# An indirect row transfer with 96 rows in place of 97, in a fused attention, Fourier and expert kernel

## The chip, the cores and the metric

The kernel runs on one core of one Trainium2 chip. The metric is the device time of one execution in microseconds (us). The core's engines are TensorE (PE), VectorE (DVE), ScalarE (ACT), GpSimd (POOL) and SyncE (SP, which here only issues transfers); each has its own instruction queue and works it off in order, and they wait for each other and for transfers by semaphores. Sixteen DMA engines carry the transfers.

## What is computed

Three parts follow each other, all in float32. Shapes: 4 batches, 8 heads, 576 tokens, head size 64, so a model width of 512; 32 memory slots; 8 experts.

```python
# attention through 32 memory slots
a = softmax(phi, axis=tokens)
k_m, v_m = einsum(a, k), einsum(a, v)                # (32, 64) for each head
attn = softmax(q @ k_m.T / 8)
x = heads_side_by_side(attn @ v_m)                   # (4, 576, 512)
# Fourier mix, then a dense feed-forward network (FFN)
u = x + real(fft(fft(x, axis=tokens), axis=model))
un = layer_norm(u)
x = u + relu(un @ w_ch1) @ w_ch2                     # 512 -> 2048 -> 512
# experts: one expert for each token, by a gate and a scan along the tokens
out[t] = p[e] * (relu(x[t] @ w1[e]) @ w2[e])         # 512 -> 1024 -> 512
```

## The kernel before

The kernel has three stages. The first (0 to about 207 us) does attention and the Fourier mix batch by batch, and meanwhile loads and prepares the weights of the FFN. The second runs the FFN over 9 groups of 256 tokens. The third runs the experts, with loops whose length the chip decides.

In the first stage the real part of the transform over the tokens is symmetric: the rows s and -s (that is 576 - s) use the same products. So for each batch b only the tokens 0 to 288 are worked, in three row blocks t = 0, 1, 2 of 97, 96 and 96 rows (`ROWS`: tokens 0-96, 97-192, 193-288), one row in each SBUF partition. The function `mix` (L495) finishes a block. It forms `ta` and `tb` (the difference and the sum of two halves of a PSUM tile, L503 and L504) and from them two result tiles:

- `ut0`, the rows s themselves. They are in order and go by ordinary transfers, issued on SP, into the segment t of `u[b]` in DRAM (L515). `spread` cuts such a transfer into the rows that make a multiple of 16 and the rest, so 97 rows go as 96 and 1.
- `ut1`, the rows -s (written by L510 and L511 in the second pass of the loop at L507). They come out in reverse order and go by one indirect transfer, issued on POOL (L520), into the segment 5 - t of `u[b]`. The list of target rows is the column t of `mi`, one number in each partition, made on the host in `constants` (L92 to L98). Two rows have no mirror image, token 0 (the first row of t=0) and token 288 (the last row of t=2); their number is 2^20, out of the bounds that the transfer is given, and such a row is not written.

The segments (`SEGS`) have 97, 96, 96, 95, 96 and 96 rows.

`ut0` and `ut1` have two buffers each. L510 of a block therefore waits until the transfer of the block two before it has left its buffer: t=2 waits for t=0's, the next batch's t=0 for t=1's.

The order of all instructions on each engine is fixed when the program is built. The loop bodies are generators that state which engine they need, for how long and after what; `weave` (L215) picks the step that starts earliest by those stated times, and what it issues is then in the engine's queue for good. For the landing of an indirect transfer it assumes 2.6 us after the issue (L519), whatever the row count.

Right behind `mix` on DVE's queue stand, from case to case, the preparation of weights (`sw`, L640 to L644), the scaled `kb` and `vb` of the next batch (L417), and in the last batch `hl`, the low half of the FFN's hidden values (L1030). PE needs `kb` for L427, and then ACT, PE and DVE follow with L430, L441, L444, L480 and `mx` (L486). The products of the FFN are at L989 to L991: `pl` of the first layer, `y` of the second. After the third block of batch 2, SP fetches the first token group's rows from `u` (L268), and DVE starts on them at L298.

Of the kernel before, what the change touches and what calls it, by code (L numbers as in the profile page):

```python
# [18 lines left out]
IO = bass.IndirectOffsetOnAxis  # L19

B, H, S_, D = 4, 8, 576, 64
# [9 lines left out]
SEGS = ((0, 97), (97, 96), (193, 96), (289, 95), (384, 96), (480, 96))  # L31
# [49 lines left out]
def constants():  # L81

    s = np.arange(289)
    ang = 2 * np.pi * np.outer(s, s) / S_
    c = np.cos(ang)
    c[0] *= 0.5
    c[288] *= 0.5
    n = np.sin(ang)
    n[[0, 288]] = 0
    n[:, [0, 288]] = 0  # L90
    cs = np.zeros((112, 3, 2, 289), np.float32)
    midx = np.full((112, 3), 1 << 20, np.int32)  # L92
    for t, (o, m) in enumerate(ROWS):
        cs[:m, t, 0] = c[o:o + m]
        cs[:m, t, 1] = n[o:o + m]
        for r in range(m):
            if 1 <= o + r <= 287:
                midx[r, t] = S_ - (o + r) - SEGS[5 - t][0]  # L98
    d = PERM[:, None] * np.arange(257)[None] * 2 * np.pi / DM
    cd = np.concatenate([np.cos(d), np.sin(d[:, 1:256])], 1).astype(np.float32)  # L100
    cd = np.ascontiguousarray(cd.reshape(4, 128, 512).transpose(1, 0, 2))
    p = np.arange(128)
    s0 = np.zeros((128, NT))
    for b in range(B):
        s0[S_ * b % 128, S_ * b // 128] = 1
    f = {
        "s0": s0,
        "tid": 128 * np.arange(NT)[None] + p[:, None] - N,
        "desc": np.tile(8 - np.arange(8), (128, 1)),
        "iotaC": np.tile(np.arange(256), (128, 1)),  # L110
        "ohR": (p[:, None] // 9 == np.arange(8)[None]) & (p[:, None] < 72),
        "kR": np.where(p < 72, p % 9, 0)[:, None],
        "ones": np.ones((128, 8)),
        "ident": np.eye(128),
        "mask": np.kron(np.eye(4), np.ones((32, 1))),
        "half": np.full((128, 1), -0.5),
        "k256": np.tile(256 * np.arange(9), (128, 1)),
        "row": p[:, None],
        "big": np.tile([768, -768], (128, 1)),
    }  # L120
    c1, c2 = (np.concatenate([f[n] for n, _ in x], 1).astype(np.float32) for x in FIELDS)
    return {"cs": cs, "cd": cd, "c1": c1, "c2": c2, "midx": midx}
# [36 lines left out]
def attention_fourier_experts_kernel(ctx, tc, qT, phi, kv, w1, w2, wg, wgc, wm, cs, cd, c1, c2, midx, out):  # L159
    nc = tc.nc  # L160
    V, S, T, G = nc.vector, nc.scalar, nc.tensor, nc.gpsimd
# [3 lines left out]
    u = [[dram.tile([n, DM], F32, name=f"u_{b}_{r}") for r, n in SEGS] for b in range(B)]  # L165
# [35 lines left out]
    def ended(*names):  # L201
        return [end.get(n, 0.0) for n in names]
# [49 lines left out]
    def spread(rows):  # L252

        n = rows - rows % 16
        return [(a, b) for a, b in ((0, n), (n, rows)) if b > a]
# [80 lines left out]
    mi = ac.tile([112, 3], I32, name="mi")  # L336
# [158 lines left out]
    def mix(b, t, xp, pq, pq_end):  # L495

        o, m = ROWS[t]
        r = yield "S", 0.27, [pq_end]
        S.copy(qs[:m, 1:256], pq[:m, 257:512])
        ta = aw.tile([97, 257], F32, name="ta")  # L500
        tb = aw.tile([97, 257], F32, name="tb")
        r = yield "V", 0.68, [r]
        V.tensor_tensor(out=ta[:m], in0=pq[:m, 0:257], in1=qs[:m], op=ALU.subtract)  # L503
        V.tensor_tensor(out=tb[:m], in0=pq[:m, 0:257], in1=qs[:m], op=ALU.add)  # L504
        mark["D"] = 3 * b + t
        end["D", 3 * b + t] = r
        for hf, (e, f) in enumerate(((ta, tb), (tb, ta))):  # L507
            ut = aw.tile([97, 512], F32, name=f"ut{hf}", bufs=2)
            r = yield "V", 0.68, ended(("sent", 3 * b + t - 2, hf))
            V.tensor_tensor(out=ut[:m, 0:256], in0=xp[hf][:m, 0:256], in1=e[:m, 0:256], op=ALU.add)  # L510
            V.tensor_tensor(out=ut[:m, 256:512], in0=xp[hf][:m, 256:512], in1=f[:m, 1:257], op=ALU.add)  # L511
            if hf == 0:
                end["sent", 3 * b + t, 0] = yield "D", 0.55, [r]
                for p, q in spread(m):
                    nc.sync.dma_start(out=u[b][t][p:q], in_=ut[p:q])  # L515
        end["mix", 3 * b + t] = r
        if t < 2 or b + 1 < B:
            mark["mix"] = 3 * b + t
        end["sent", 3 * b + t, 1] = 2.6 + (yield "G", 1.04, [r])  # L519
        G.indirect_dma_start(out=u[b][5 - t], out_offset=IO(ap=mi[:m, t:t + 1], axis=0), in_=ut[:m],  # L520
                             in_offset=None, bounds_check=SEGS[5 - t][1] - 1, oob_is_err=False)
        mark["mix"] = 3 * b + t

# [2 lines left out]
    def mixer():  # L526
        for n in range(3 * B):
            yield lambda: len(mixes) > n
            yield float(BATCH["mix"][n // 3])
            yield from mix(*mixes[n])  # L530
# [753 lines left out]
```

## Time and profile before

| | before |
|---|---|
| median of 3 runs | 925.37 us (923.09 to 926.46) |
| the profiled execution | 925.92 us |
| its span (first to last instruction) | 924.2 us |
| PE busy | 827.2 us (90%) |
| DVE busy | 617.2 us (67%) |
| ACT busy | 317.3 us (34%) |
| POOL busy | 214.7 us (23%) |
| software queue of the transfers (q0) | 7472 packets, 14.02 MB |

The profile is that of one execution. All times in it are counted from the start of the span. The busy shares are means over the three stages: PE's 90% is 144.63 us of the first 207 and 473.24 us of the 483 us from 207 to 690 us. What one stage is worth is read from its own rows. An indirect transfer appears twice: as POOL's time to issue it, and as a landing, the time from the start of the issue to the last row's arrival. Where the profile could tell a landing for sure, it gives one.

### The profile page before, as it was taken

To read this page: it belongs to the slowest core of one execution; us is meant where nothing else is said; L and a number is where in the kernel's file an instruction comes from. 1 tells how busy PE (TensorE), PEld (TensorE's weight loads), DVE (VectorE), ACT (ScalarE), POOL (GpSimd) and SP (SyncE) were. 2 spreads that over 40 slices of the span, in tenths; PEclk is the share of its full clock that TensorE was granted. 3 is DMA by queue.
4 is the path that set the end of the run, shared out by engine and by line. 5 is a ranking of instruction groups with operands and counts; after the bars stand their busy time and mean duration, and the time that the engine had idled before them with its cause. 6 is when DMAs were issued, how large, how long until landed. Compare 5 with 4: busy or idle time off the path is not lost. (4 is left out here: it accounts for less than half of the span.)

```text
span 924.2 us, 14424 instructions
## 1 busy us (share of the span) xinstructions
PE 827.2 (90%) x5296; PEld 703.4 (76%) x5296; DVE 617.2 (67%) x1422; ACT 317.3 (34%) x595; POOL 214.7 (23%) x179
## 2 busy tenths in 40 slices
PE   5594959568899999999999999999998998999993
PEld 2353636357789989898989898988987997889973
DVE  3984956469987665757575757577865666766654
ACT  3452624235431111111111111115344555645543
POOL 0544544337410000000000000003323331333330
PEclk9787978799899999999999999999998999999997
DMA  9865632344240100000000000019366667866665
GB/s 333 280 216 148 242 88 64 102 141 147 76 164 1 47 24 24 24 24 24 23 25 24 24 23 18 6 56 356 132 212 209 218 220 264 285 222 232 223 214 188
DMA packets 38714, 123.43 MB, mean 134 GB/s; under 512 B 8096, under 2 KB 8352, under 8 KB 36826
## 3 DMA queue, kind: packets, MB, share of 16 engines
q1 hardware_dynamic: 29880, 103.22, 33.5%
q0 software_dynamic: 7472, 14.02, 4.7%
q10 hardware_dynamic: 1266, 4.98, 1.5%
q8 instruction: 52, 0.85, 0.4%
q14 instruction: 44, 0.36, 0.1%
HBM read 107.41 MB, written 15.57 MB: 133 GB/s over the span
## 5 line engine op out<-in xcount | busy, mean ns | idle before, releaser
L991 PE MATMUL pl<-xh,w1l 128*128 128x256 f32 x864 | 243.3, 282 | 0.0
L989 PE MATMUL pl<-xh,w1h 128*128 128x256 f32 x576 | 163.5, 284 | 3.7 <-DVE hl L1030 3.7
L991 PEld LDWEIGHTS pl<-xh,w1l 128*128 128x128 f32 x864 | 164.5, 190 | 0.0
L990 PE MATMUL pl<-xl,w1h 128*128 128x256 f32 x576 | 161.8, 281 | 0.0
L1028 ACT ACTIVATE hh<-pl 128x256 fp32r<-128x256 f32 x144 | 55.1, 384 | 306.8 <-PE pl L991 279.6
L991 PE MATMUL y<-w2h,hl 128*128 128x512 f32 x288 | 114.1, 396 | 7.7 <-DVE hl L1030 7.7
L1162 DVE TENSOR_TENSOR w1l<-w1h,w2h 128x1024 fp32r<-128x1024 f32 x89 | 107.6, 1221 | 19.2 <-ACT w2h L1160 13.1
L1160 ACT CAST w2h<-w1h 128x1024 fp32r<-128x1024 f32 x100 | 103.5, 1049 | 40.6 <-issue 31.6
L989 PE MATMUL y<-w2h,hh 128*128 128x512 f32 x288 | 116.8, 406 | 0.0
L990 PE MATMUL y<-w2l,hh 128*128 128x512 f32 x288 | 114.0, 396 | 2.2 <-DVE w2l L660 2.2
L989 PEld LDWEIGHTS pl<-xh,w1h 128*128 128x128 f32 x576 | 109.1, 189 | 8.5 <-DVE hl L1030 4.6
L990 PEld LDWEIGHTS pl<-xl,w1h 128*128 128x128 f32 x576 | 109.6, 190 | 3.6
L1030 DVE SCALAR_TENSOR_TENSOR hl<-pl,hh 128x256 fp32r<-128x256 f32 x144 | 60.3, 421 | 72.5 <-ACT hh L1028 72.4
L752 DVE SCALAR_TENSOR_TENSOR jk<-stg,wgt 128x512 bf16<-128x512 f32 x144 | 99.0, 687 | 2.6
L989 PE MATMUL pl<-xh,w2h 128*128 128x256 f32 x288 | 82.8, 287 | 0.0
L990 PE MATMUL pl<-xl,w2h 128*128 128x256 f32 x288 | 81.6, 283 | 0.0
L302 POOL TENSOR_TENSOR rv<-rv,C 128x1 f32<-128x1 f32 x18 | 12.0, 669 | 294.4 <-DVE rv L300 289.1
L991 PEld LDWEIGHTS y<-w2h,hl 128*128 128x128 f32 x288 | 54.6, 190 | 20.8 <-DVE hl L1030 8.5
L989 PE MATMUL y<-w2h,w2l 128*128 128x512 f32 x168 | 67.7, 403 | 0.0
L991 PE MATMUL y<-w2h,w2l 128*128 128x512 f32 x168 | 66.2, 394 | 0.0
L990 PE MATMUL y<-w1l,w2l 128*128 128x512 f32 x168 | 66.1, 393 | 0.0
L990 PEld LDWEIGHTS y<-w2l,hh 128*128 128x128 f32 x288 | 54.9, 191 | 10.5 <-DVE w2l L660 2.9
(228 smaller groups left out, 1450.5 us busy)
## 6 DMA issues: line engine op xcount, KB each, us to landing
w1h<-in_wm_dram SPq DMA_DIRECT2D x108, 512.0 KB
stg<-in_w_dram SPq DMA_DIRECT2D x29, 512.0 KB
kvt<-in_kv_dram SPq DMA_DIRECT2D x8, 1290.0 KB
ys<-stg SPq DMA_DIRECT2D x9, 520.0 KB
qt<-in_qT_dram SPq DMA_DIRECT2D x4, 1156.0 KB
ph<-in_phi_dram SPq DMA_DIRECT2D x8, 320.0 KB
u<-ut SPq DMA_DIRECT2D x12, 192.0 KB
wgt<-in_wg_dram ACTq DMA_DIRECT2D x1, 2304.0 KB
```

The lines of the kernel that those rows point to most:

```text
L302: G.tensor_tensor(out=rv, in0=rv, in1=c_("half"), op=ALU.pow)
L752: V.scalar_tensor_tensor(out=jk, in0=yt[:, t, 0:512], scalar=1.0, in1=wgt[:, e], op0=ALU.mult, op1=ALU.mult, accum_out=L[:, t, e:e + 1])
L989: T.matmul(ps, a[0], b[0], start=first, stop=False)
L990: T.matmul(ps, a[0], b[1], start=False, stop=False)
L991: T.matmul(ps, a[1], b[0], start=False, stop=last)
L1028: S.activation(out=hh, in_=ps, func=AF.Relu)
L1030: V.scalar_tensor_tensor(out=hl, in0=ps, scalar=0.0, in1=f32(hh), op0=ALU.max, op1=ALU.subtract)
L1160: S.copy(WH[c], RAW[c])
L1162: E[mark["eng"]].tensor_tensor(out=WL[c], in0=RAW[c], in1=f32(WH[c]), op=ALU.subtract)
```

## The change

For t=0 the indirect transfer takes the rows 1 to 96 of `ut1` (partitions 1 to 96) in place of the rows 0 to 96, and the list of target rows moves up by one partition, so that the entry of row r stands in partition r - 1. The row of token 0, which the transfer did not write before, is no longer in it. The same rows are written to the same places. The transfers of t=1 and t=2 stay as they were. The tile `mi` keeps its size; its last entry of t=0 is then not used.

No engine's queue gains, loses or moves an instruction: row for row the built program is the same on all five queues, but for the operands of four instructions on POOL, one in each batch, whose row count goes from 97 to 96. The transfer of t=1 has 96 indices, 96 source rows and a segment of 96 rows; t=0's has the same counts after the change, and its source starts at partition 1.

```diff
@@ constants
         for r in range(m):
             if 1 <= o + r <= 287:
-                midx[r, t] = S_ - (o + r) - SEGS[5 - t][0]
+                midx[r - (t == 0), t] = S_ - (o + r) - SEGS[5 - t][0]
@@ mix
         end["sent", 3 * b + t, 1] = 2.6 + (yield "G", 1.04, [r])
-        G.indirect_dma_start(out=u[b][5 - t], out_offset=IO(ap=mi[:m, t:t + 1], axis=0), in_=ut[:m],
+
+        a = 1 if t == 0 else 0
+        G.indirect_dma_start(out=u[b][5 - t], out_offset=IO(ap=mi[:m - a, t:t + 1], axis=0), in_=ut[a:m],
                              in_offset=None, bounds_check=SEGS[5 - t][1] - 1, oob_is_err=False)
```

## Rows read from the trace of the kernel before

**Rows 1.** DVE's timeline: start us, us, engine, line, operation [idle before <-releaser]

```profile
84.78 0.42 DVE L510 TENSOR_TENSOR ut<-pbk,tb 96x256 f32<-96x256 f32 x1 [10.87 <-DMA u<-ut,mi]
...
128.73 0.42 DVE L510 TENSOR_TENSOR ut<-pbk,tb 96x256 f32<-96x256 f32 x1 [7.22 <-DMA u<-ut,mi]
...
173.81 0.42 DVE L510 TENSOR_TENSOR ut<-pbk,tb 96x256 f32<-96x256 f32 x1 [10.45 <-DMA u<-ut,mi]
...
206.89 0.42 DVE L510 TENSOR_TENSOR ut<-pbk,tb 96x256 f32<-96x256 f32 x1 [7.25 <-DMA u<-ut,mi]
```

**Rows 2.** POOL's timeline, issues of the indirect transfer L520 (six of twelve)

```profile
68.65 2.34 POOL L520 DMA_INDIRECT u<-ut,mi  x1 [0.21 <-DVE ta L503]
...
85.81 0.92 POOL L520 DMA_INDIRECT u<-ut,mi  x1 [9.80 <-DVE ut L511]
...
113.81 2.19 POOL L520 DMA_INDIRECT u<-ut,mi  x1 [0.18 <-issue]
...
120.27 0.95 POOL L520 DMA_INDIRECT u<-ut,mi  x1 [0.16 <-DVE ta L503]
...
158.79 2.19 POOL L520 DMA_INDIRECT u<-ut,mi  x1 [0.18 <-DVE ta L503]
...
191.27 2.22 POOL L520 DMA_INDIRECT u<-ut,mi  x1 [1.26 <-DVE ut L511]
```

**Rows 3.** Landings of L520's transfers issued at 158.79, 163.59 and 85.81 us

```profile
DMA to landing us min/median/max: 15.0/15.0/15.0
...
DMA to landing us min/median/max: 10.6/10.6/10.6
...
DMA to landing us min/median/max: 2.8/2.8/2.8
```

**Rows 4.** Software queue, 80-82 and 87-88 us: packets, MB, share of 16 engines

```profile
q0 software_dynamic: 11, 0.05, 5.5%
...
q0 software_dynamic: 53, 0.19, 63.5%
```

**Rows 5.** PE's timeline, restarts after idle time in batches 0, 1 and 3

```profile
88.16 1.12 PE L427 MATMUL pfr<-C,kb 128*128 128x128 f32 x4 [11.57 <-DVE kb L417]
...
129.93 0.69 PE L427 MATMUL pfr<-C,kb 128*128 128x128 f32 x2 [7.83 <-DVE kb L417]
...
208.02 0.80 PE L991 MATMUL y<-w2h,hl 128*128 128x512 f32 x1 [7.52 <-DVE hl L1030]
```

**Rows 6.** Windows: us, busy PE, PEld, DVE, ACT, POOL, PEclk, DMA share, GB/s

```profile
88.00:92.00 4.00, 3.80 (x18) 2.80 (x18) 3.00 (x7) 1.67 (x6) 1.46 (x2) 0.50 0.74 215
...
113.00:121.00 8.00, 6.20 (x28) 3.05 (x26) 7.72 (x19) 3.45 (x7) 7.23 (x7) 1.00 0.36 94
...
130.00:134.00 4.00, 3.96 (x17) 2.57 (x18) 2.98 (x6) 1.72 (x7) 1.49 (x2) 0.50 0.17 49
...
142.00:146.00 4.00, 4.00 (x13) 3.01 (x12) 1.38 (x2) 1.15 (x3) 0.00 (x0) 0.50 0.00 0
...
175.00:179.00 4.00, 4.00 (x9) 2.80 (x9) 3.90 (x5) 0.92 (x2) 2.14 (x2) 0.50 0.51 136
...
208.00:212.00 4.00, 3.98 (x10) 3.16 (x11) 3.93 (x5) 0.62 (x1) 3.27 (x4) 0.55 0.22 60
```

**Rows 7.** DVE's timeline, the first `mx` after the restarts of batches 0 and 1

```profile
99.17 0.68 DVE L486 TENSOR_REDUCE mx<-sc 97x16 f32<-97x512 f32 x1
...
144.29 0.69 DVE L486 TENSOR_REDUCE mx<-sc 97x16 f32<-97x512 f32 x1 [2.89 <-PE sc L480]
```

**Rows 8.** Timelines of SP and DVE: the first token group's rows

```profile
163.74 5.95 SPq L268 DMA_DIRECT2D u<-u  x8
...
179.61 0.69 DVE L298 BATCH_NORM_STATS2 bs<-u 128x6 f32<-128x512 f32 x1
```

**Rows 9.** Windows of the FFN, columns as in rows 6

```profile
216.00:260.00 44.00, 36.98 (x218) 32.46 (x219) 42.06 (x57) 25.41 (x46) 23.11 (x17) 0.92 0.40 118
...
300.00:600.00 300.00, 300.00 (x1971) 270.36 (x1970) 189.79 (x603) 47.49 (x121) 8.14 (x12) 1.00 0.07 24
```

## The prediction

> **What bounds the kernel now.** I read four views in this order: VectorE's (DVE's) timeline over the attention and Fourier stage (0 to 207 us), the timeline of GpSimd (POOL) with the landings of its transfers, TensorE's (PE's) timeline, and busy time with the granted clock by windows. The stage behind it, from 300 to 600 us, has PE busy for 300.00 of 300.00 us at clock 1.00 [rows 9]: nothing there waits for anything, so a change in the start of that stage moves its end by as much. The question is what sets its start.
>
> DVE has four long holes, one in each batch: 10.87, 7.22, 10.45 and 7.25 us, 35.79 us together, each ahead of L510 and each ended by the landing of `u<-ut,mi`, the indirect transfer of L520 [rows 1]. The buffer explains it. `ut1` has two buffers, so the third row block of a batch (t=2) writes the buffer that the first (t=0) gave to its transfer, and must wait until that has landed. It is t=0's transfer that is late. POOL needs 2.34, 2.19, 2.19 and 2.22 us to issue it, but 0.92 or 0.95 us for one of t=2 or t=1 [rows 2]. t=0's of batch 2 lands 15.0 us after its issue, t=1's behind it 10.6 us after its own, while t=2's of batch 0, alone, takes 2.8 us [rows 3]. The DMA view says why: between 80 and 82 us the software queue moves 11 packets in 5.5% of sixteen engines' time, which is 0.055 x 16 = 0.9 of one engine; t=2's rows between 87 and 88 us are 53 packets at 63.5%, some ten engines at once [rows 4]. The 97 rows go through one engine, 96 rows through all.
>
> While DVE stands, the rest stands too: PE sits idle 11.57 us in batch 0 and 7.83 us in batch 1 until `kb` (queued on DVE right behind the waiting L510 and L511), and 7.52 us at 208.02 until `hl` [rows 5]. So this wait is on the path of every batch.
>
> **The change, part by part.** No instruction is added, removed or moved; four transfers change their operands.
>
> (a) *The transfer itself.* It gets the count of t=1's: 96 indices, 96 source rows, a target block of 96 rows. Nothing in the trace starts such a source at partition 1 rather than 0; the nearest row is t=1's, and I take its form. Its issue costs 0.95 us instead of 2.2 us, four times 1.25 us on POOL; POOL waits for DVE (9.80 us idle ahead of the issue at 85.81 [rows 2]), so I count nothing for it. If that idle time were gone, it would be worth up to 5 us more.
>
> (b) *The wait.* How early must the transfer land? DVE reached the waiting L510 at its start less its hole: 73.91, 121.51, 163.36 and 199.64 us [rows 1]; the issues stand at 68.65, 113.81, 158.79 and 191.27 us [rows 2]. That leaves 5.26, 7.70, 4.57 and 8.37 us. With 2.8 us to land, nothing of the wait is left. With 10.6 us, the slow end (a 96-row transfer queued behind others), 5.3 + 2.9 + 6.0 + 2.2 = 16.4 us stay. I take the value near the fast end, since the 10.6 us were spent behind t=0's own transfer, and leave 1 us in all for batches 0 and 2, where weights and q are loading. Gain: 35.8 - 1 = 34.8 us.
>
> [...]
>
> (c) *What is late next.* Batch 0 and 1: `kb`, then PE's and ACT's work on it, whose inputs were there before; the shift passes whole. Batch 2: SP fetches the rows of the first token group from 163.74 to 169.69 us, and DVE's statistics on them start at 179.61 us [rows 8]. Moved up by 10.45 us they would start at 169.2 us, before the last fetch was even issued; landing takes another 2 to 3 us, as the 2.8 us above. The fetches do not wait for L520, so they do not move with it. I take 2 us lost here. In batch 3 the FFN's first loads (its constants, the second half of the weights) are issued from the same queues; their landings are not in the rows, and I take another 2 us, between 0 and the whole 7.25 us. Together 4 us.
>
> (d) *PE's clock.* [...] I take 8 us; the bounds are 0 (the clock falls anyway) and 13.9 us (PE sets the pace everywhere).
>
> Sum: 34.8 - 4 + 8 = 38.8 us. The profiled execution took 925.92 us (span 924.2 us), so 925.92 - 38.8 = 887 us. It stands 0.55 us above the median of 925.37 us, which changes nothing here.
>
> **The rivals.**
> 1. *The cause is not the count, or a source that starts at partition 1 is served as badly.* Then DVE waits as before: 925 us. Against it: t=1 and t=2 differ from t=0 in little else, and t=2's list also has a row that is not written (row 288), so the unwritten row is not the cause. Chance 0.06.
> 2. *The transfer stays slow beside the loads.* All batches get the 10.6 us: the gain is 35.8 - 16.4 = 19.4 us, without the clock, 906 us (902 to 916). For it: traffic in a shorter stage gets denser. Against it: 2.8 us where it was alone [rows 3], and all engines at once for 96 rows [rows 4]. Chance 0.09.
> 3. *The FFN's first group falls to the low clock (slower than before).* From 216 to 260 us PE is busy 36.98 of 44 us at 0.92 [rows 9], paced by the weights that DVE and POOL prepare. If the front passes time on so that PE meets more gaps there, up to 37 us of its work could take twice as long: 925.9 - 34.8 + 4 + 37 = 932 us. It decides from the point where over 38 us are lost there or in the front. Against it: the order and the preparation move along with PE, so the gaps stay what they are. Chance 0.02.
> 4. *More than forecast*: all 35.8 us, the whole 13.9 us and POOL's time, below 877 us. Chance 0.03.
>
> **How the numbers follow.** The forecast, 877 to 902 us, has 0.80: its upper end is half of the 16.4 us left, 4 us late and no clock gained (35.8 - 8.2 - 4 = 23.6 us, 902 us), its lower end the whole wait and most of the clock. That is also the range. A measurement of this kernel can tell some 0.5% (4.6 us) from no change. Faster by more: 0.80 + 0.09 + 0.03 = 0.92; within: 0.06; slower: 0.02.
>
> **What would show it.** Four issues of L520 for t=0 near 0.95 us and a landing near 3 us; no row "L510 waits for u<-ut,mi" above 2 us in DVE's waits; the `y` product of 208.02 us some 39 us earlier; windows at 0.50 gone between 78 and 180 us; PE full from about 260 us on, as before. The forecast is wrong if the holes stay (rival 1), if DVE waits at the same places for other loads (a leak in step c larger than 4 us), or if PE's windows are still at 0.50 (step d).

## The result and the profile after

The kernel after takes 887.79 us, median of four runs (886.43 to 890.97), against 925.91 us of the kernel before on the same chip: a ratio of 0.958, 95% interval 0.952 to 0.964. The forecast was 887 us in a range of 877 to 902. In a second comparison on another chip the same kernel took 883.18 us against 930.20, ratio 0.951 (0.945 to 0.957). The gain is thus 38 us in the first comparison and 47 us in the second, and most of the 9 us between them is not the change's: the stretches measured below differ by 1.3 us.

The profiled execution took 890.97 us, span 889.1 us. The lines of the DVE timeline that answer to [rows 1] no longer have a bracket: nothing was waited for ahead of L510 of t=2. (The lines of the kernel after from the change on are two higher.)

```profile
77.93 0.41 DVE L510 TENSOR_TENSOR ut<-pbk,tb 96x256 f32<-96x256 f32 x1
...
115.64 0.41 DVE L510 TENSOR_TENSOR ut<-pbk,tb 96x256 f32<-96x256 f32 x1
...
142.54 0.41 DVE L510 TENSOR_TENSOR ut<-pbk,tb 96x256 f32<-96x256 f32 x1
...
168.41 0.41 DVE L510 TENSOR_TENSOR ut<-pbk,tb 96x256 f32<-96x256 f32 x1
```

In POOL's timeline t=0's issues, as in [rows 2], fell from 2.2 to about 1 us:

```profile
73.15 1.11 POOL L522 DMA_INDIRECT u<-ut,mi  x1 [0.18 <-DVE ta L503]
...
106.32 0.95 POOL L522 DMA_INDIRECT u<-ut,mi  x1 [0.16 <-issue]
...
138.46 0.95 POOL L522 DMA_INDIRECT u<-ut,mi  x1 [0.16 <-DVE ta L503]
...
160.10 0.99 POOL L522 DMA_INDIRECT u<-ut,mi  x1 [1.23 <-DVE ut L511]
```

The view of line L522 gives the landings on record, against up to 15.0 us in [rows 3]:

```profile
DMA to landing us min/median/max: 2.8/3.2/5.3
```

DVE's waits between 60 and 210 us (us in total, times, longest) were led by 35.8 us for `u<-ut,mi`. That row is gone, and the one that leads now is short:

```profile
DVE mx L486 <- PE sc L480: 4.2, 4, 2.0
```

The first four windows, with the columns of [rows 6], stand on PE's work behind the places of the four holes. The last answers to the window of [rows 9] from 216 to 260 us: the product `y` with `hl` that stood at 208.02 us [rows 5] now stands at 169.54 us, so the window begins 38.5 us earlier. The granted clock is the figure behind the five engines:

```profile
80.00:84.00 4.00, 3.08 (x26) 1.99 (x22) 3.83 (x10) 2.09 (x8) 2.28 (x2) 1.00 0.89 283
...
118.00:122.00 4.00, 4.00 (x23) 2.08 (x23) 2.60 (x6) 2.99 (x9) 1.27 (x1) 1.00 0.40 88
...
143.00:147.00 4.00, 3.97 (x22) 3.12 (x21) 3.90 (x6) 1.89 (x6) 3.10 (x4) 1.00 0.73 214
170.00:174.00 4.00, 4.00 (x28) 3.60 (x27) 3.90 (x6) 1.01 (x2) 3.27 (x4) 1.00 0.85 253
...
177.50:221.50 44.00, 36.28 (x220) 31.79 (x219) 41.34 (x56) 26.32 (x47) 23.48 (x18) 0.96 0.47 146
```

The clock is 1.00 where 0.50 stood before. What this is worth, the stretch from `kb` on PE to the first `mx` on DVE shows, in batches 0 and 1. It took 99.17 - 88.16 = 11.01 and 144.29 - 129.93 = 14.36 us before [rows 5, 7], with the clock at 0.50 until 92 us in the one and, by the windows from 127 to 146 us, all along in the other. Now it takes 91.71 - 81.79 = 9.92 and 125.00 - 116.34 = 8.66 us, the same within 0.01 us in the second execution of the kernel after (9.93 and 8.66). The rows of PE's timeline

```profile
81.79 0.83 PE L427 MATMUL pfr<-C,kb 128*128 128x128 f32 x4 [0.65 <-DVE kb L417]
...
116.34 0.93 PE L427 MATMUL pfr<-C,kb 128*128 128x128 f32 x4
```

and of DVE's:

```profile
91.71 0.68 DVE L486 TENSOR_REDUCE mx<-sc 97x16 f32<-97x512 f32 x1
...
125.00 0.68 DVE L486 TENSOR_REDUCE mx<-sc 97x16 f32<-97x512 f32 x1
```

**A measure for the part that the change touches.** Executions of one kernel differ by several us in places that the change cannot reach. So I measure each profiled execution by one stretch on DVE: from the first L511 of batch 0 to L298 of the FFN's third token group. These are its two ends in DVE's timeline of the kernel before,

```profile
65.82 0.41 DVE L511 TENSOR_TENSOR ut<-pbk,tb 97x256 f32<-97x256 f32 x1
...
278.48 0.69 DVE L298 BATCH_NORM_STATS2 bs<-u 128x6 f32<-128x512 f32 x1
```

of the kernel after,

```profile
70.35 0.41 DVE L511 TENSOR_TENSOR ut<-pbk,tb 97x256 f32<-97x256 f32 x1
...
238.73 0.69 DVE L298 BATCH_NORM_STATS2 bs<-u 128x6 f32<-128x512 f32 x1
```

and of the kernel after in a second profiled execution (e9_after):

```profile
64.71 0.41 DVE L511 TENSOR_TENSOR ut<-pbk,tb 97x256 f32<-97x256 f32 x1
...
231.81 0.69 DVE L298 BATCH_NORM_STATS2 bs<-u 128x6 f32<-128x512 f32 x1
```

The stretch is 212.66 us before, 168.38 us after and 167.10 us in the second execution of after: 44.3 and 45.6 us shorter. These are single executions; e1_95 below, which has no hole either, has 169.41 us, so the stretch without holes varies by some 2 us; with all four holes e4_warm, the kernel before with idle work added on PE, has 212.26 us. The first profiled execution of after gave 4.5 us away ahead of the stretch (its first L511 stands at 70.35 instead of 65.82 us) and 4.7 us behind it (889.1 - 238.73 = 650.4 us, before 924.2 - 278.48 = 645.7 us). The second gave away neither: 64.71 us, and 876.5 - 231.81 = 644.7 us.

### The profile page after: what moved, and what is told of

It reads as the page before. It is cut to its first block, busy times and chain, and to the rows that moved or that the text cites. A ratio compares the mean times of both kernels' runs of the same rounds, so it can differ in the third digit from the quotient of the medians.

```text
span 889.1 us, 14424 instructions
## 1 busy us (share of the span) xinstructions
PE 820.6 (92%) x5296; PEld 700.2 (79%) x5296; DVE 616.5 (69%) x1422; ACT 316.9 (36%) x595; POOL 209.4 (24%) x179
## 3 DMA queue, kind: packets, MB, share of 16 engines
q1 hardware_dynamic: 29880, 103.22, 34.7%
## 4 chain that ended last, share of the span: by engine, by line
PE 64%; DMA 13%; DVE 11%; issue 8%; ACT 2%; POOL 1%; POOLq 0%; SPq 0%; DVEq 0%
PE pl L991 9%; PE y L991 9%; PE pl L992 9%; PE y L992 9%; PE pl L993 9%; PE y L993 9%; DMA out_dram<-u,idx 6%; DMA stg<-ys,idx 2%; DVE sw L644 2%; PE pt L281 2%; PE pbk L570 1%; DVE sw L646 1%; DVE sw L642 1%; DMA kvt<-in_kv_dram 1%; DMA cdt<-in_cd_dram 1%
```

## The experiments

Each kernel ran beside the kernel before on one chip. The medians of the kernel before were 925.9 to 933.5 us in the five comparisons, so the ratio and the stretch say more than the time. (The ratio is the one on record with its interval; it is not the quotient of the two medians. A stretch is that of the one profiled execution.)

| kernel | base | us | ratio to before (95%) | stretch, us | shorter than before by |
|---|---|---|---|---|---|
| before | | 925.9 to 933.5 | | 212.66 | |
| after | | 887.79 | 0.958 (0.952 to 0.964) | 168.38 | 44.3 |
| e9_after | after, again | 883.18 | 0.951 (0.945 to 0.957) | 167.10 | 45.6 |
| e1_95 | after | 886.33 | 0.948 (0.938 to 0.957) | 169.41 | 43.3 |
| e7_112 | before | 891.72 | 0.960 (0.953 to 0.967) | 170.97 | 41.7 |
| e2_split | before | 906.60 | 0.970 (0.960 to 0.981) | 188.59 | 24.1 |
| e3_buf3 | before | 899.10 | 0.962 (0.953 to 0.971) | 177.98 | 34.7 |
| e10_un96 | after | 885.44 | 0.944 (0.940 to 0.948) | 169.64 | 43.0 |
| e4_warm | before | 925.79 | 0.998 (0.993 to 1.002) | 212.26 | 0.4 |
| e8_b0 | after | 900.62 | 0.967 (0.961 to 0.972) | 186.95 | 25.7 |
| e5_b1 | after | 895.64 | 0.964 (0.956 to 0.971) | 179.44 | 33.2 |
| e6_b2 | after | 892.93 | 0.961 (0.953 to 0.968) | 176.00 | 36.7 |
| e8_b3 | after | 894.25 | 0.962 (0.957 to 0.967) | 176.75 | 35.9 |

### Is it the count?

Three kernels change the number of rows in other ways than the change did.

**e7_112.** More rows, the unwritten one among them, source from partition 0:

```diff
-            ut = aw.tile([97, 512], F32, name=f"ut{hf}", bufs=2)
+            ut = aw.tile([112 if hf else 97, 512], F32, name=f"ut{hf}", bufs=2)
...
+            if hf == 1 and t == 0:
+                V.memset(ut[96:112], 0.0)
...
-        G.indirect_dma_start(out=u[b][5 - t], out_offset=IO(ap=mi[:m, t:t + 1], axis=0), in_=ut[:m],
+        z = 112 if t == 0 else m
+        G.indirect_dma_start(out=u[b][5 - t], out_offset=IO(ap=mi[:z, t:t + 1], axis=0), in_=ut[:z],
```

> On the kernel before the change: t=0's transfer keeps its unwritten row and starts at partition 0, and gets more rows rather than fewer: 112, of which the 15 added ones have an index out of bounds and are not written (DVE clears them first, 16 x 512 values in each batch). Theory 1 (what counts is by how many DMA engines the number of rows can be shared out; 112 is 16 x 7, as 96 is 16 x 6): the issue takes about 1 us, the landing 3 to 5 us, the packets go over all engines, the holes ahead of L510 are gone, and the time is 886 to 894 us. Rival 1 (an unwritten row in the list, or the source's start, is what is slow) and a rival by which more rows simply take longer: issue 2.2 us or more, holes as before, 925 us or more.

POOL's timeline shows the first of t=0's four issues (the others took 0.97 to 1.17 us):

```profile
70.12 1.13 POOL L523 DMA_INDIRECT u<-ut,mi  x1 [0.61 <-DVE ut L513]
```

The view of its line has the landings on record, of t=0, 1 and 2 together:

```profile
DMA to landing us min/median/max: 2.9/3.1/5.7
```

No hole is left, and the kernel takes 891.72 us. So neither the unwritten row in the list nor the place where the source starts was what made t=0 slow, nor do more rows take longer: the slowest landing of this view is 5.7 us, the 97 rows of [rows 3] took 15.0. Rival 1 of the prediction falls here.

**e1_95.** On the kernel after, t=2 gets 95 rows:

```diff
-        G.indirect_dma_start(out=u[b][5 - t], out_offset=IO(ap=mi[:m - a, t:t + 1], axis=0), in_=ut[a:m],
+        z = m - 1 if t == 2 else m
+        G.indirect_dma_start(out=u[b][5 - t], out_offset=IO(ap=mi[:z - a, t:t + 1], axis=0), in_=ut[a:z],
```

> On the kernel after the change: t=2 leaves out its unwritten row as well, 95 rows instead of 96. Theory 1 (the number of rows decides how many DMA engines share the transfer; 96 is what helps, not that a row is left out): t=2's issue rises from 0.95 us to between 1.2 and 2.2 us, its landing from some 3 us to between 5 and 12 us, and its packets are spread over fewer engines. The time stays at 885 to 892 us, since the next writer of that buffer, the next batch's t=1, comes some 30 us later. Rival 1 (it helps that the row which is not written is left out): issue 0.95 us or less, landing 3 us or less, the time unchanged. [...]

The first of t=2's issues, from POOL's timeline:

```profile
80.34 1.38 POOL L523 DMA_INDIRECT u<-ut,mi  x1 [0.20 <-issue]
```

All landings on record, from the view of the line:

```profile
DMA to landing us min/median/max: 2.8/3.7/8.1
```

t=2's four transfers now take 8.1, 4.6, 5.4 and 7.1 us to land and 1.15 to 1.38 us to issue; with 96 rows they were issued in 0.92 to 1.26 us, and those on record took 4.7 to 5.3 us beside loads (batches 0 and 3) and 3.0 us without (batch 1, e9_after). These lie at the lower end of what theory 1 expected or just below it, and against rival 1: leaving the unwritten row out made it worse. The time did not move, as nobody waits for these landings.

**e2_split.** On the kernel before, the 97 rows in two transfers:

```diff
-        G.indirect_dma_start(out=u[b][5 - t], out_offset=IO(ap=mi[:m, t:t + 1], axis=0), in_=ut[:m],
-                             in_offset=None, bounds_check=SEGS[5 - t][1] - 1, oob_is_err=False)
+        for p, q, col in ((0, 64, 0), (64, 97, 3)) if t == 0 else ((0, m, t),):
+            G.indirect_dma_start(out=u[b][5 - t], out_offset=IO(ap=mi[:q - p, col:col + 1], axis=0), in_=ut[p:q],
+                                 in_offset=None, bounds_check=SEGS[5 - t][1] - 1, oob_is_err=False)
```

> On the kernel before the change: t=0's transfer keeps all its 97 rows, the unwritten one too, and the source starts at partition 0, but it is sent as two transfers, of 64 and of 33 rows. Theory 1 (a transfer of 97 rows goes through one engine): both halves are issued in about 1 us each and have landed 3 to 5 us after their issue; the four holes ahead of L510 (35.8 us) are gone, and the time is 885 to 895 us. Rival 1 (the unwritten row, or where the source starts, is what counts): holes as before, 925 us, or longer for the added issue.

The landings came nearly as expected (2.7 to 3.6 us for 64 rows; 5.3 and 2.7 us for the two on record with 33). The time did not. The two halves write the same block of `u`, and POOL holds the second back until the first has landed (the trace names this wait in batches 1, 2 and 3, 6.5 us together); in batches 0 and 2 a hole of 4.68 and 2.17 us stays, and `mx` waits for a PE at 0.50 (the window 86 to 90 us). A row of POOL's timeline,

```profile
119.14 0.92 POOL L523 DMA_INDIRECT u<-ut,mi  x1 [2.00 <-DMA u<-ut,mi]
```

the two holes in DVE's,

```profile
81.79 0.42 DVE L512 TENSOR_TENSOR ut<-pbk,tb 96x256 f32<-96x256 f32 x1 [4.68 <-DMA u<-ut,mi]
...
157.07 0.42 DVE L512 TENSOR_TENSOR ut<-pbk,tb 96x256 f32<-96x256 f32 x1 [2.17 <-DMA u<-ut,mi]
```

and the longest of DVE's waits between 60 and 250 us:

```profile
DVE mx L488 <- PE sc L482: 10.9, 6, 4.2
```

So its landings speak for the count. Its 906.60 us miss the expectation by some 12 us, since I had not seen the order of the two halves. Of the 20 us by which its stretch is longer than the kernel after's, the two holes are 6.9 us. The rest stands beside them as longer waits for PE and ACT and a clock at 0.50 in the windows from 82 to 90 and from 98 to 102 us, and no run divides it.

Put together, t=0's landings on record are 14.0 to 18.7 us with 97 rows (all runs that have them), 2.8 to 3.7 with 96, 3.0 and 3.2 with 112, and 2.7 to 3.6 with 64. t=2's are longer with 95 rows than with 96 in each of the three batches on record (above). So the landing goes with the count and not with its size: 64, 96 and 112, the quick ones, are multiples of 16, and 97 and 95 are not. That the rows are shared out among the engines by such a number is theory 1 of e7_112; how many engines were at work was read for 97 and 96 rows alone [rows 4].

### Is the landing's wait the whole price?

**e3_buf3** leaves the slow transfer and takes the wait away; **e10_un96** does the same edit on the kernel after, to tell what the buffer itself costs:

```diff
-            ut = aw.tile([97, 512], F32, name=f"ut{hf}", bufs=2)
+            if hf == 1 and t == 2:
+                ut = stg1.tile([128, 512], F32, name="un")
+            else:
+                ut = aw.tile([97, 512], F32, name=f"ut{hf}", bufs=2)
```

> On the kernel before the change: the transfer of t=0 is left as it is (97 rows, 2.2 us of issue, 10 to 15 us to landing), but t=2 writes its second half into a buffer of its own (the tile un, idle in this stage), so DVE does not wait for t=0's landing. Theory 1 (the wait for the landing is the whole price of the slow transfer; POOL's issue time costs nothing): no hole ahead of L510 of t=2, issue and landing of t=0 as before, 887 to 897 us. Rival 2 (POOL's longer issue and the crowded queue have a price of their own): the holes gone, but 905 to 925 us, with waits for POOL or for the rows that t=1 and t=2 send behind t=0's.

> On the kernel after the change (96 rows, quick transfers): t=2 writes its second half into the tile un all the same, as in the run with a buffer of its own on the kernel before. It tells what of the 10 us, by which that run stayed behind the kernel after, belongs to sharing the tile un with the token groups behind it, and what to the slow transfers. Theory 1 (the slow transfers have a second price, through the loads that queue behind them): the time is that of the kernel after within 3 us (880 to 892 us), the front from batch 0 to the FFN gains 43 to 45 us, and DVE waits for no load of C or u. Rival 4 (sharing un is the price): 895 to 900 us, the front gains 34 to 37 us, with the same waits as in that run.

In e3_buf3 the twelve landings are as slow as ever (t=0's are 18.7, 15.0, 15.0 and 15.0 us, and t=1's behind them 14.8, 9.0, 10.6 and 11.4), and the holes are gone. The view of the line:

```profile
DMA to landing us min/median/max: 7.0/12.1/18.7
```

In place of the holes DVE's waits between 60 and 250 us name transfers that it waits for neither in the kernel before nor in the kernel after:

```profile
DVE tri L1129 <- DMA C<-in_c_dram: 2.5, 1, 2.5
DVE pm L376 <- DMA ph<-in_phi_dram: 2.2, 1, 2.2
...
DVE bs L298 <- DMA C<-in_c_dram: 1.6, 1, 1.6
...
DVE un L304 <- DMA u<-un,mi: 1.1, 1, 1.1
DVE bs L298 <- DMA u<-u: 0.6, 1, 0.6
```

Its stretch gains 34.7 us; with the same buffer and 96 rows it gains 43.0. So the wait at L510 was some four fifths of the price. The four slow transfers cost 43.0 - 34.7 = 8.3 us more once nobody stands still for them. The waits listed add up to 8.0 us: a load of `phi` in the first stage (2.2 us), the FFN's first loads (4.7 us) and the shared tile's own transfer (1.1 us) are waited for while slow transfers are under way or have just landed. The granted clock is lower there as well, 0.956 in the mean of the profiled execution against e10_un96's 0.974, and no run separates the two. The 899.10 us lie between the two ranges expected, nearer to theory 1's. Sharing `un` costs little: e10_un96 has a time between the two of the kernel after and a stretch 1.3 us above the longer one, with no wait for a load of `C` or `u`, as theory 1 expected. A price of POOL's longer issue by itself is shown by no row of the two.

### What does the clock cost?

**e4_warm** gives PE something to do in the first two holes of the kernel before:

```diff
+                for c in range({(2, 0, 0): 80, (3, 0, 1): 55}.get((b, i, g), 0)):
+                    T.transpose(pt[:, g, 0], id_, id_)
```

> On the kernel before the change: while DVE stands in the holes of batches 0 and 1, PE is given work that nobody needs (80 transposes of a constant ahead of kb in the front part of batch 2, 55 in that of batch 3). The holes stay. Theory 1 (the low clock behind the holes has a price of its own, 7 to 8 us in the four batches, most of it in batch 1): the granted clock behind the first two holes stays near 1.00 and the time is 914 to 921 us. Rival 3 (the clock is a by-product, and ACT and DVE set the pace behind a hole): the clock stays near 1.00 and the time is 923 to 928 us. If the clock falls all the same, nothing is told apart.

PE's timeline has it busy for 8.90 us of the first hole,

```profile
76.39 8.90 PE L427 MATMUL pfr<-C 128*128 128x128 f32 x80
```

and still the clock fell, only later, by the windows (columns of [rows 6]):

```profile
92.00:96.00 4.00, 4.00 (x12) 1.36 (x10) 2.67 (x3) 2.08 (x5) 0.66 (x1) 0.50 0.90 317
...
134.00:138.00 4.00, 4.00 (x14) 1.32 (x12) 1.88 (x4) 2.61 (x6) 1.27 (x1) 0.50 0.38 98
```

From `kb` to `mx` batch 0 took 12.87 us (11.01 before), batch 1 12.66 us (14.36 before). In batch 0 the clock is 0.50 from 92 to 96 us and 0.58 from 96 to 100 us, where it was back at 1.00 before; in batch 1 it is 0.94 from 130 to 134 us and 0.78 from 142 to 146 us, both 0.50 before [rows 6]. The time of each batch went with it. The two cancel, and the run as a whole tells nothing apart, as the expectation said of this case.

**e8_b0, e5_b1, e6_b2, e8_b3** answer it better: each is the kernel after, with the old 97-row form in one batch alone (here batch 1; the old list stands in a fourth column of `mi`):

```diff
-        a = 1 if t == 0 else 0
-        G.indirect_dma_start(out=u[b][5 - t], out_offset=IO(ap=mi[:m - a, t:t + 1], axis=0), in_=ut[a:m],
+        a = 1 if t == 0 and b != 1 else 0
+        col = 3 if t == 0 and b == 1 else t
+        G.indirect_dma_start(out=u[b][5 - t], out_offset=IO(ap=mi[:m - a, col:col + 1], axis=0), in_=ut[a:m],
```

> On the kernel after the change: t=0's transfer of batch 0 alone goes with 97 rows again. Theory 1 (each hole passes whole, and the clock behind it adds what it costs): the hole of 10.9 us comes back in batch 0, and the front is 11 to 12.5 us longer than in the kernel after. Rival (part of the shift was lost anyway to the loads behind): under 10 us. In the time, against the kernel after in the same comparison: 11 to 13 us more.

> On the kernel after the change: t=0's transfer of batch 1 alone goes with 97 rows again. Theory 1 (hole and low clock behind it are two prices): the hole of some 7.2 us ahead of L510 comes back in batch 1, PE restarts at 0.50, and the time is 885 to 889 us for the kernel after, plus 7.2 us, plus some 3 to 7 us of clock: 897 to 903 us. Rival 3 (the clock is a by-product): the hole alone, 894 to 896 us. Batches 0, 2 and 3 stay without a hole.

> On the kernel after the change: t=0's transfer of batch 2 alone goes with 97 rows again. Theory 1 (a hole passes whole to the end, and nothing else is late next): the hole of some 10.5 us comes back in batch 2, the time is 10 to 12 us over that of the kernel after, 897 to 901 us. The prediction's step c (2 us of this batch's hole are lost to the loads of the first token group): 8 to 8.5 us over, 895 to 896.5 us. Batches 0, 1 and 3 stay without a hole.

> On the kernel after the change: t=0's transfer of batch 3 alone goes with 97 rows again. Theory 1 (nothing of this hole is lost to the FFN's first loads, and the low clock behind it has a price): 7.25 us of hole and 1 to 1.5 us of clock, 8 to 9 us more than the kernel after. The prediction's step c (2 us of this hole lost to the FFN's first loads): 5 to 6.5 us more.

Each hole comes back where it was put: 10.7, 7.15, 9.49 and 6.9 us (and alone, but for 0.59 us in batch 0 of e5_b1). DVE's wait in e8_b0 (us, times, longest),

```profile
DVE ut L512 <- DMA u<-ut,mi: 10.7, 1, 10.7
```

the hole in DVE's timeline of e5_b1,

```profile
117.54 0.42 DVE L512 TENSOR_TENSOR ut<-pbk,tb 96x256 f32<-96x256 f32 x1 [7.15 <-DMA u<-ut,mi]
```

that of e6_b2,

```profile
147.17 0.42 DVE L512 TENSOR_TENSOR ut<-pbk,tb 96x256 f32<-96x256 f32 x1 [9.49 <-DMA u<-ut,mi]
```

and DVE's wait in e8_b3:

```profile
DVE ut L512 <- DMA u<-ut,mi: 6.9, 1, 6.9
```

The price of each is its stretch less 168.3 us, the mean of the three executions without a hole (after, e9_after, e1_95): batch 0 18.7 us, batch 1 11.1, batch 2 7.7, batch 3 8.5. Together 45.9 us, against the 44.4 us that all four give at once. The three executions behind the mean differ by 2.3 us, so a price is good to one or two us. The medians say the same more roughly. On e9_after's chip, where it took 883.18 us, batch 0 costs 17.4 us and batch 3 11.1 us, both more than any expectation. e5_b1's 895.64 us lie in rival 3's range and not in theory 1's, and e6_b2's 892.93 us lie below both of its ranges; these two had no kernel after on their chip, and here the stretch and the rows of the clock decide. Three points follow.

First, holes and clock are two prices. In e5_b1 batch 1 needs 132.08 - 118.74 = 13.3 us from `kb` to `mx` instead of 8.66, with the clock at 0.50 from 117 to 129 us. In e8_b0 batch 0 needs 102.03 - 87.24 = 14.8 us instead of 9.92, with the clock at 0.50 from 84 to 92 and from 96 to 100 us and at 0.52 from 100 to 104 us. A window and the row of `mx` of e5_b1,

```profile
121.00:125.00 4.00, 4.00 (x14) 1.35 (x12) 1.22 (x3) 2.61 (x6) 1.27 (x1) 0.50 0.42 130
...
132.08 0.69 DVE L488 TENSOR_REDUCE mx<-sc 97x16 f32<-97x512 f32 x1 [1.86 <-PE sc L482]
```

and of e8_b0:

```profile
96.00:100.00 4.00, 4.00 (x12) 1.67 (x10) 1.77 (x3) 1.72 (x4) 0.04 (x1) 0.50 0.31 64
...
102.03 0.69 DVE L488 TENSOR_REDUCE mx<-sc 97x16 f32<-97x512 f32 x1 [4.19 <-PE sc L482]
```

Second, the clock's price is not fixed by the hole. Batch 0 of the kernel before has the same hole, and needed only 11.01 us there, since the clock came back at 92 us. That is most of why e8_b0 missed its expectation of 11 to 12.5 us by 6. PE was slow once more, in a place without a hole: the same eight products `pbk` took 3.62 us from 163.62 us and 1.89 us from 169.58 us.

Third, batch 2 costs less than its hole: 7.7 us, near the 8 to 8.5 us that step (c) expected and not the 10 to 12 of theory 1. But of the 1.8 us between hole and price 1.06 us is found in one instruction, for another reason than the one that step (c) gave; the next section has it. The rest is within the spread.

**e9_after** is the kernel after without an edit.

> The kernel after the change once more, beside the three above on the same chip, to compare them with it and to see which of its differences from the kernel before are the same in a second profiled execution. Theory 1: 885 to 891 us; between the first L511 of batch 0 and the FFN the same 44 us gained as in the first execution, holes 35 us and the rest clock. If the 4.5 us lost in the first 62 us and the 4 us lost near 790 us belong to the change, they are there again; if they belong to the one execution, they are not.

Its two ends of the stretch stand above. The 4.5 us ahead of the stretch and the 4.7 us behind it are not there again, and e3_buf3, with the old transfers, has the late first L511 as well (69.43 us). They belong to the one execution and not to the change. For the first the clock shows more: in after it is 0.50 from 45 to 61 us, in before 0.50 from 45 to 51 us and 1.00 from 52 us on. The second execution's 883.18 us lie a little below the expected 885 to 891 us.

## Why the prediction was right, and where it was not

**What bounds the kernel.** Right. The holes are t=0's landings, seen through the buffer: taking the buffer away (e3_buf3) and taking the count of 97 away (e7_112, e2_split) each remove them, wholly or for the most part.

**(a) The transfer.** Right: 0.95 to 1.11 us to issue, and 2.8 and 3.0 us to land where the landing is on record. With DVE at work beside most of them, the twelve issues of the kernel after took 0.92 to 1.26 us.

**(b) The wait.** Right, and a little too careful: no residue in either profiled execution of after, where 1 us was left for it. The 10.6 us of t=1, which were the slow bound, were time behind t=0: its landings on record now take 3.2 us in after and 2.8 to 5.2 us in e9_after.

**(c) What is late next: 4 us. Wrong in size and place.** That the fetches of the first token group do not move with batch 2's hole is right: they begin 71.6 us after the first L511 in e6_b2, which has that hole, and 72.7 and 71.2 us after it in the two executions of after. What failed is which fetch DVE waits for. The prediction let the statistics wait for the last of the eight. By the code (`load_u`, L257) the first four bring the rows of the first L298, and the other four those of the second. The four had been issued 14.2 us ahead of the first L298 [rows 8], so 10.45 us less would have left 3.8 us. In the kernel after 149.38 - 145.34 = 4.0 us are left, the second L298 follows at 155.37 us, and DVE waits at neither. SP's timeline has the first four before

```profile
163.74 1.65 SPq L268 DMA_DIRECT2D u<-u  x4
```

and after,

```profile
143.00 2.34 SPq L268 DMA_DIRECT2D u<-u  x4
```

and DVE's timeline has the two L298 of the kernel after:

```profile
149.38 0.69 DVE L298 BATCH_NORM_STATS2 bs<-u 128x6 f32<-128x512 f32 x1
...
155.37 0.69 DVE L298 BATCH_NORM_STATS2 bs<-u 128x6 f32<-128x512 f32 x1
```

The last of the eight is late only beside the slow transfer: SP took 5.37 to 5.96 us over the eight in the four executions with 97 rows in batch 2, and 3.45 to 4.25 us in the nine others.

What batch 2 did lose is 1.06 us, in an instruction that stood right behind the hole. L642 (L640 before, L645 in e6_b2), the first step on the weights, takes 1.47 us in both executions of the kernel after, where POOL works on two `eo` beside it, and 0.41 us in e6_b2 and before (at 174.48 us), where the hole has given POOL time to finish them. The timeline of the kernel after

```profile
142.96 0.74 POOL L470 TENSOR_TENSOR eo<-at 96x256 f32<-96x256 f32 x1
143.21 1.47 DVE L642 TENSOR_SCALAR sw<-stg 128x512 uint32<-128x512 uint32 x1
143.65 0.73 POOL L471 TENSOR_TENSOR eo<-at 96x256 f32<-96x256 f32 x1
```

and that of e6_b2:

```profile
147.84 0.41 DVE L645 TENSOR_SCALAR sw<-stg 128x512 uint32<-128x512 uint32 x1
```

The ends of DVE's step and of POOL's second one, 143.21 + 1.47 and 143.65 + 0.73, are 0.3 us apart; why the one is longer beside the other, no run here was made to test. In batch 3 nothing was lost: its hole of 6.9 us costs 8.5 us of the stretch in e8_b3, as theory 1 expected, not the 5 to 6.5 us of step (c).

**(d) The clock: 8 us. Right that it has a price, a little small.** No run shows the 8 us, nor the bound of 13.9 us, as such; the runs show this in their place. From the stretches, what is left beside the holes and the 1.06 us is 44.28 - 35.79 + 1.06 = 9.6 us in the one execution and 45.56 - 35.79 + 1.06 = 10.8 us in the other. Between `kb` and `mx` alone it is (11.01 - 9.92) + (14.36 - 8.66) = 6.8 us; the other 3 to 4 us go to the clock by what is left, and no row shows them as its price. At 1.00 the two batches need 9.92 and 8.66 us, so they are not alike but for the clock. For each us of a stretch at 0.50 the price was (14.8 - 9.9) / 14.8 = 0.33 us in e8_b0 and 5.7 / 14.4 = 0.40 us in batch 1 of the kernel before. How long 0.50 lasts behind a hole is not fixed by the hole: behind that of batch 0 it lasts until 92 us in before and until about 104 us in e8_b0.

**The sum.** With the measured terms it is 35.8 - 1 + 10 = 44.8 us, 881 us from the profiled execution. Here the 1 us is the instruction beside POOL, and 10 us is all that the stretches leave to the clock. The forecast's 38.8 us were 6 us too few: 3 by step (c), 2 by step (d) and 1 by step (b). That the first median came out at 887.79 us, within 1 us of the forecast, owes something to chance: the second comparison's 883.18 us is nearer to the sum of the measured terms. Both lie in the range. The mark that the prediction named, the product `y` with `hl` of 208.02 us [rows 5], stands at 169.54 us in the first execution, 38.5 us earlier with 4.5 us already lost ahead of it. Of its other signs one held only in the second execution of after: in the first, 0.50 stood once between 78 and 180 us (109.6 to 113.0 us), in a place without a hole. Of the rivals, the first is refuted (e7_112), the second too (no landing of 10.6 us is left), and the third's point was not reached (its low clock is the 0.50 of [rows 6]): in the window that answers to that of [rows 9] PE is busy 36.28 of 44 us at 0.96, before 36.98 at 0.92. The fourth's 877 us were not reached by either median.

## What to carry to other kernels

Count the rows of an indirect transfer before its bytes: 97 rows took some five times as long to land as 96 or 112 (14.0 to 18.7 us against 2.8 to 3.7), and padding up (with out-of-bounds indices) served almost as well as leaving one out. When a wait is taken away, ask of each load behind it which instruction needs which part: the first statistics needed four of the eight fetches, and these were early enough. Compare kernels whose executions differ by several us over the stretch that a change can reach, not over the whole span.

## What the runs showed of the hardware that I had not expected

A transfer of 97 rows brings packets that carry next to nothing. The software queue over the whole span (packets, MB, share), before

```profile
q0 software_dynamic: 7472, 14.02, 4.7%
```

and after:

```profile
q0 software_dynamic: 4528, 14.00, 4.7%
```

That is 2944 packets fewer, 736 for each of the four transfers, with 0.02 MB in all of them. One 97-row transfer in e8_b0 brings exactly 736 more than after (5264), four of 95 rows in e1_95 4 x 112 more (4976), four of 112 rows 4 x 16 (4592).

The clock fell at places without a hole, too, and not at the same places in two executions of one kernel: before had it at 0.50 from 235.5 to 242.3 us, after from 109.6 to 113.0 us and from 188.1 to 191.6 us, and e9_after has 1.00 in the windows from 60 to 173, 181 to 225 and 260 to 560 us. The two executions of after differ by 5.6 us ahead of the stretch and by 5.7 us behind it, more than some of the terms of the prediction.
